# A decode attention kernel: a quarter of the score products moved from TensorE to VectorE, and the exponentials and value products moved later

## The chip, the cores and the metric

One core of a Trainium2 chip runs the kernel. The metric is device time in microseconds (us), with the median over the runs of one kernel. Before the change the kernel took 1358.11 us (median of 4 runs, 1356.54 to 1359.36).

Engine names are those of the profile: PE is TensorE's matmuls, PEld its weight loads, DVE is VectorE, ACT is ScalarE, POOL is GpSimd, and SP issues the large DMA transfers.

## The reference

It is one decode step: one query token against a cache of 65536 keys, with grouped heads, plus a small feed-forward branch.

```python
B, Sq, D = 1, 1, 448
Hq, Hkv, Sk, Dh = 16, 8, 65536, 256      # all bf16
xn = layernorm(x)
q = (xn @ wq)                            # 16 heads of 256
k, v = repeat(k_cache, 2), repeat(v_cache, 2)      # each K/V head serves 2 query heads
p = softmax(q @ k.T * Dh**-0.5)
out = x + (p @ v) @ wo + B(xn)           # B: one gated feed-forward (448 -> 1792 -> 448) on the token
```

The K and V caches are 268 MB each and every byte is used once. Nothing else is near that size: all the weights together are about 12 MB.

## The kernel before

Each of the 8 K/V heads is a head group `g`. Its keys come in 16 chunks of 4096 keys (2 MB of K, 2 MB of V), so there are 128 chunks `i` in all. K and V have three chunk buffers each. One chunk holds 32 tiles of 128 keys.

```python
T = 32; CK = 128 * T; NCH = SK // CK     # 16 chunks per head group
GRP = 4; GPC = T // GRP                  # 8 groups of 4 key tiles per chunk
NKB = 3; NVB = 3; NSLOT = 4; LAG = 3
PV_SLACK = 16
PV_OFF = GPC * NCH + PV_SLACK            # V runs 144 groups = 18 chunks behind K
def _evac_engine(kg): return 1 if (kg % 8) in (2, 6) else 0     # 1: ScalarE, 0: VectorE
```

The kernel first transposes K on TensorE: keys lie on partitions, and the product sums over the 256 head dimensions. For each group it does 8 transposes into a PSUM bank; VectorE or ScalarE copies the bank to SBUF (an eviction, `KTsb`); then TensorE does 8 score products with the two query heads. Scores of a chunk are copied to `Ssb`. The value products of chunk `i - 18` stand between the groups.

```python
# TensorE, for each step n
    if vg % GPC == 0: do_pv_chunk(iv)    # 64 products with V chunk iv
    do_tr(n)                             # 8 transposes of group n
    if n >= LAG: do_qk(n - LAG)          # waits for the eviction of group n-3
```

After 16 chunks VectorE takes the maximum per partition, GpSimd reduces it over partitions, and ScalarE does the exponentials. ScalarE takes its work in program order:

```python
# ScalarE
for kg in range(NG):
    if evac_eng[kg] == 1:
        act.wait_ge(sem_tr, kg + 1)
        ...
        act.copy(KTsb[:, kg % NSLOT, :], kt_ps_bank(kg % NSLOT)).then_inc(sem_eact, 1)
        while exp_next[0] < HKV and kg >= GPC * NCH * (exp_next[0] + 1) + 2:
            do_exp(exp_next[0])          # waits for GpSimd's maximum of that head group
            exp_next[0] += 1
```

SP issues a K chunk when the buffer it goes into is free, that is when all transposes of the chunk three before are done; a V chunk when the products of the V chunk three before are done. `wq` borrows two V buffers at the start.

```python
# SP
if kind == 0:
    if i >= NKB: sp.wait_ge(sem_kfree, i - NKB + 1)
    ... sp.dma_start(Kbuf[:, b, :], src).then_inc(sem_kd[b], 16)
else:
    if i >= NVB: sp.wait_ge(sem_vfree, i - NVB + 1)
    elif b in (0, 1): sp.wait_ge(sem_pe, P_Q)
    ... sp.dma_start(Vbuf[:, b, :], src).then_inc(sem_vd[b], 16)
```

## Time and profile before

| | before |
|---|---|
| span of the profiled run | 1356.7 us |
| busy: PE / DVE / ACT | 81% / 42% / 20% |
| moved by DMA | 552.41 MB |
| DMA rate in most slices | 424 to 428 GB/s |

First the page of the kernel before. The first line is busy time and its share of the span. The next two are the span in 40 equal slices (33.9 us each): the busy share of the 16 DMA engines in tenths, and what they moved. The q lines are DMA queues: packets, MB, share of the 16 engines' time; q8 and q14 fetch the engines' instructions. The L lines are groups of instructions: count, busy time, mean ns of one, and the idle time before them with what ended it.

```profile
PE 1098.2 (81%) x24872; PEld 1069.6 (79%) x24872; DVE 569.6 (42%) x928; ACT 276.7 (20%) x297; POOL 12.2 (1%) x30
...
DMA  9999699999999999999999999999999999999797
GB/s 345 412 411 394 244 427 424 425 425 426 426 424 423 426 405 426 424 424 424 425 425 426 419 374 428 424 423 427 421 426 424 425 422 390 425 425 398 290 417 319
...
q8 instruction: 195, 3.19, 0.9%
q14 instruction: 20, 0.16, 0.0%
...
L473 PE MATMUL ps<-identb,Kbuf 128*128 128x128 bf16 x8192 | 792.5, 254 | 90.7 <-DMA Kbuf<-in_A_k_cache_dram 52.9
L315 DVE COPY KTsb<-ps 128x1024 bf16<-128x1024 bf16 x768 | 521.2, 691 | 513.0 <-PE ps L473 511.0
...
L387 ACT COPY KTsb<-ps 128x1024 bf16<-128x1024 bf16 x256 | 258.9, 1011 | 877.1 <-PE ps L473 877.1
```

PE has the highest busy share of the compute engines, but the DMA row is full and flat. If all 552.41 MB had moved at 425.5 GB/s, it would have taken 1298 us. The span is 59 us longer. As long as the kernel moves these bytes at this rate, only those 59 us can be won, so the first question is where they lie. The Trainium skill (DMA: Bandwidth & Descriptors, "Where 436 GB/s comes from") gives 435.2 GB/s as the ceiling of the 16 ports into SBUF; the flat 424 to 428 GB/s of these slices agrees with being close to it. The same section says that about 358 GB/s, the HBM side, binds for transfers from HBM. It reckons that figure as half of what two cores share; one core alone read 549.03 MB from HBM at 405 GB/s over the whole span here, so for a lone core that limit does not hold in this case.

Next, windows of the kernel before. Columns: the stretch, its length, then busy time and instruction count of each engine, the granted TensorE clock, the DMA engines' busy share, GB/s.

```profile
0.00:60.00 60.00, 28.28 (x391) 23.15 (x392) 13.41 (x25) 5.47 (x10) 7.19 (x14) 1.00 0.96 375
60.00:146.00 86.00, 81.63 (x1984) 80.67 (x1982) 65.17 (x110) 32.00 (x32) 0.00 (x0) 1.00 1.00 402
146.00:180.00 34.00, 22.43 (x517) 22.24 (x515) 13.60 (x24) 8.32 (x11) 0.63 (x2) 0.75 0.64 255
180.00:1240.00 1060.00, 905.25 (x20445) 891.02 (x20443) 466.01 (x751) 225.16 (x237) 3.75 (x12) 0.77 1.00 421
1240.00:1280.00 40.00, 24.33 (x613) 23.80 (x610) 10.59 (x19) 5.76 (x8) 0.63 (x2) 0.64 0.72 286
1280.00:1340.00 60.00, 28.44 (x747) 22.49 (x744) 0.00 (x0) 0.00 (x0) 0.00 (x0) 0.56 1.00 422
1340.00:1356.70 16.70, 7.79 (x198) 6.20 (x198) 0.83 (x3) 0.00 (x0) 0.00 (x0) 0.50 0.49 207
```

I call "time short" the length of a stretch times (1 - its rate / 425.5). It is 7.1, 4.7, 13.6, 11.2, 13.1, 0.5 and 8.6 us for these seven lines, 58.8 us together. In the middle line most of it, 9 us, is in three short holes (slices 15, 23/24 and 34).

The cause of the holes is seen in the timeline around 146 us: start, length, engine, line, instruction, and in brackets the idle time before it and what ended that.

```profile
146.21 0.38 POOL L244 PARTITION_ALL_REDUCE gmax<-pmax  x1 [137.98 <-DVE pmax L307]
148.24 0.61 PE L473 MATMUL ps<-identb,Kbuf 128*128 128x128 bf16 x8
157.47 0.25 POOL L246 TENSOR_SCALAR negmax<-gmax 128x2 f32<-128x2 f32 x1 [10.88 <-issue]
157.75 0.87 ACT L373 ACTIVATE Psb<-Ssb,negmax 128x512 bf16<-128x512 f32 x1 [11.10 <-POOL negmax L246]
159.37 0.99 ACT L387 COPY KTsb<-ps 128x1024 bf16<-128x1024 bf16 x1
160.42 0.37 PE L496 MATMUL ps<-qT,KTsb 128*128 128x2 bf16 x8 [11.57 <-ACT KTsb L387]
```

GpSimd's reduction over partitions takes 11 us here until its result is used (7 to 11 us over the eight head groups). ScalarE reaches the exponential at once and stands there for 11.1 us. The next eviction is behind it in ScalarE's program, and TensorE stands for 11.6 us behind that eviction. All K and V buffers are full then, so the DMA queue stops. The list of waits has this line (total us, times, longest). Seven of the eight are the first seven head groups, with 11.7 us for the first and 4 to 8 us for the others; the eighth is 0.2 us:

```profile
PEld ps L496 <- ACT KTsb L387: 44.0, 8, 11.7
```

### The profile page before, as it was taken

How to read it: one execution, taken by the hardware profiler on the slowest of the kernel's cores; microseconds unless marked ns; L12 is line 12 of the kernel's file. 1: busy time of each engine (PE TensorE's matmuls, PEld its weight loads, DVE VectorE, ACT ScalarE, POOL GpSimd, SP SyncE). 2: the span in 40 equal slices, each digit the busy share in tenths (PEclk: the TensorE clock that was granted, in tenths of full speed). 3: DMA queues.
4: the chain of work that ended last, by engine and by line, in shares of the span. 5: the costliest groups of instructions: out<-in, count | busy, mean ns of one | idle time of the engine just before them, and what ended most of it. 6: DMA issues, size and time to landing. Idle time of an engine off the chain costs nothing.

```text
span 1356.7 us, 52498 instructions
## 1 busy us (share of the span) xinstructions
PE 1098.2 (81%) x24872; PEld 1069.6 (79%) x24872; DVE 569.6 (42%) x928; ACT 276.7 (20%) x297; POOL 12.2 (1%) x30
## 2 busy tenths in 40 slices
PE   3789698897899788887888878898788879888463
PEld 3689698887889788887788878898788879887443
DVE  2378444444444444444444344444344444444100
ACT  0133221222122122212212122221222122121100
POOL 2000000000000000000000000000000000000000
PEclk9999777877777778878877768767788677778565
DMA  9999699999999999999999999999999999999797
GB/s 345 412 411 394 244 427 424 425 425 426 426 424 423 426 405 426 424 424 424 425 425 426 419 374 428 424 423 427 421 426 424 425 422 390 425 425 398 290 417 319
DMA packets 39341, 552.41 MB, mean 407 GB/s; under 512 B 4259, under 2 KB 4294, under 8 KB 5910
## 3 DMA queue, kind: packets, MB, share of 16 engines
q1 hardware_dynamic: 37382, 540.56, 94.9%
q0 software_dynamic: 1744, 8.49, 1.6%
q8 instruction: 195, 3.19, 0.9%
q14 instruction: 20, 0.16, 0.0%
HBM read 549.03 MB, written 0.00 MB: 405 GB/s over the span
## 4 chain that ended last, share of the span: by engine, by line
PE 52%; DMA 35%; issue 9%; ACT 1%; DVE 1%; POOLq 1%; POOL 1%; ACTq 0%
PE ps L473 33%; DMA Kbuf<-in_A_k_cache_dram 27%; PE ps L496 10%; PE ps L529 8%; DMA Vbuf<-in_A_v_cache_dram 4%; DMA wd_sb<-in_B_w_down_dram 3%; POOLq L77 1%; DVE pmax L307 1%; PE ps L551 1%; ACT Psb L373 1%; ACT KTsb L387 1%; PE ps L439 0%; POOL gmax L244 0%; DVE KTsb L315 0%; DVE Ssb L301 0%
## 5 line engine op out<-in xcount | busy, mean ns | idle before, releaser
L473 PE MATMUL ps<-identb,Kbuf 128*128 128x128 bf16 x8192 | 792.5, 254 | 90.7 <-DMA Kbuf<-in_A_k_cache_dram 52.9
L315 DVE COPY KTsb<-ps 128x1024 bf16<-128x1024 bf16 x768 | 521.2, 691 | 513.0 <-PE ps L473 511.0
L473 PEld LDWEIGHTS ps<-identb,Kbuf 128*128 128x128 bf16 x8192 | 594.3, 114 | 94.8 <-DMA Kbuf<-in_A_k_cache_dram 56.9
L387 ACT COPY KTsb<-ps 128x1024 bf16<-128x1024 bf16 x256 | 258.9, 1011 | 877.1 <-PE ps L473 877.1
L496 PE MATMUL ps<-qT,KTsb 128*128 128x2 bf16 x8192 | 374.1, 166 | 61.3 <-ACT KTsb L387 42.1
L496 PEld LDWEIGHTS ps<-qT,KTsb 128*128 128x128 bf16 x8192 | 356.7, 104 | 71.4 <-ACT KTsb L387 44.0
L529 PE MATMUL ps<-Psb,Vbuf 128*128 128x2 bf16 x8192 | 229.4, 164 | 61.4 <-DMA Vbuf<-in_A_v_cache_dram 37.9
L529 PEld LDWEIGHTS ps<-Psb,Vbuf 128*128 128x128 bf16 x8192 | 218.8, 97 | 65.0 <-DMA Vbuf<-in_A_v_cache_dram 38.9
L301 DVE COPY Ssb<-ps 128x64 f32<-128x64 f32 x128 | 28.8, 225 | 134.8 <-PE ps L473 134.4
L336 DVE TENSOR_TENSOR OTsb<-ps,rrec 128x2 bf16<-128x2 f32 x2 | 0.2, 154 | 74.4 <-PE ps L529 74.4
L373 ACT ACTIVATE Psb<-Ssb,negmax 128x512 bf16<-128x512 f32 x16 | 13.4, 859 | 85.2 <-POOL negmax L246 85.2
L421 PE MATMUL ps<-xnT,Vbuf 128*128 128x1 bf16 (+1 forms) x128 | 9.2, 174 | 10.5 <-DMA Vbuf<-in_A_wq_dram 10.5
L421 PEld LDWEIGHTS ps<-xnT,Vbuf 128*128 128x128 bf16 (+1 forms) x128 | 8.3, 106 | 11.4 <-issue 10.5
L244 POOL PARTITION_ALL_REDUCE gmax<-pmax x8 | 3.0, 375 | 1188.5 <-DVE pmax L307 1188.5
L285 DVE TENSOR_TENSOR gs_sb<-ps,sig_sb 128x14 f32<-128x14 f32 x1 | 0.2, 174 | 29.8 <-ACT sig_sb L360 29.8
L439 PE MATMUL ps<-wd_sb,hT_b 128*1 128x448 bf16 x14 | 4.7, 517 | 9.2 <-DMA wd_sb<-in_B_w_down_dram 9.2
L439 PEld LDWEIGHTS ps<-wd_sb,hT_b 128*1 128x1 bf16 x14 | 1.5, 114 | 12.0 <-issue 11.9
L307 DVE TENSOR_REDUCE pmax<-Ssb 128x2 f32<-128x1024 f32 x8 | 9.8, 1220 | 0.3
L551 PE MATMUL ps<-wo_sb,OTsb 128*1 128x448 bf16 x32 | 9.7, 477 | 0.0
L566 PE MATMUL ps<-rowsum,onesf 128*128 128x16 f32 x2 | 0.6, 386 | 11.0 <-ACT Psb L373 11.0
L566 PEld LDWEIGHTS ps<-rowsum,onesf 128*128 128x128 f32 x2 | 0.5, 313 | 11.1 <-ACT Psb L373 11.1
L551 PEld LDWEIGHTS ps<-wo_sb,OTsb 128*1 128x1 bf16 x32 | 3.2, 104 | 5.3 <-issue 4.0
(55 smaller groups left out, 45.9 us busy)
## 6 DMA issues: line engine op xcount, KB each, us to landing
Kbuf<-in_A_k_cache_dram SPq DMA_DIRECT2D x128, 2048.0 KB, 19.9
Vbuf<-in_A_v_cache_dram SPq DMA_DIRECT2D x128, 2048.0 KB, 23.2
wo_sb<-in_A_wo_dram POOLq DMA_DIRECT2D x1, 3584.0 KB, 76.1
Vbuf<-in_A_wq_dram SPq DMA_DIRECT2D x3, 1024.0 KB, 8.2
wd_sb<-in_B_w_down_dram POOLq DMA_DIRECT2D x1, 1568.0 KB, 43.7
wg_sb<-in_B_w_gate_dram POOLq DMA_DIRECT2D x1, 1344.0 KB, 12.7
wu_sb<-in_B_w_up_dram POOLq DMA_DIRECT2D x1, 1344.0 KB, 23.4
Vbuf<-in_A_wq_dram SPq DMA_DIRECT2D x1, 512.0 KB, 16.5
```

The costliest lines, as they stand in the source:

```text
L77: with ExitStack() as es, nc.Block() as block:
L301: dve.tensor_copy(Ssb[:, g % 2, s * 2 * T:(s + 1) * 2 * T], s_ps_chunk(i)).then_inc(sem_sevac, 1)
L307: dve.tensor_reduce(pmax[:, 2 * g:2 * g + 2], sv, AX.X, ALU.max).then_inc(sem_smdve, 1)
L315: dve.tensor_copy(KTsb[:, kg % NSLOT, :], kt_ps_bank(kg % NSLOT)).then_inc(sem_edve, 1)
L373: ins = act.activation(pv[:, h, :], sv[:, h, :], ACTF.Exp, bias=negmax[:, 2 * g + h:2 * g + h + 1], scale=1.0, accum_out=rowsum[:, 2 * g + ...
L387: act.copy(KTsb[:, kg % NSLOT, :], kt_ps_bank(kg % NSLOT)).then_inc(sem_eact, 1)
L421: ins = pe.matmul(ps[:, col:col + 1], lhsT=wq_view(c, kc)[:, h16 * DH + a * 128:h16 * DH + a * 128 + 128], rhs=xnT[0:kc, c:c + 1], start=( ...
L439: ins = pe.matmul(ps[0:1, YC:YC + D_MODEL], lhsT=hT_b[:, f:f + 1], rhs=wd_sb[:, f, :], start=(f == 0), stop=(f == NFC - 1))
L473: ins = pe.transpose(kt_ps(bank, 2 * tl + a), src, identb[:, :])
L496: ins = pe.matmul(s_ps(i2, t), lhsT=KTsb[:, slot, (2 * tl + a) * 128:(2 * tl + a + 1) * 128], rhs=qT[:, a * 16 + 2 * g:a * 16 + 2 * g + 2] ...
L529: ins = pe.matmul(ot_ps(gv, a), lhsT=Vbuf[:, b, t * DH + a * 128:t * DH + a * 128 + 128], rhs=Psb[:, gv % 2, s * 2 * T + 2 * t:s * 2 * T + ...
L551: ins = pe.matmul(ps[0:1, YAC:YAC + D_MODEL], lhsT=OTsb[:, col:col + 1], rhs=wo_sb[:, c, :], start=(first and k == 0), stop=(last and k == ...
```

## The change

It has two parts. First, VectorE scores some key tiles directly: it multiplies 128 keys x 256 values by a q row that lies on every partition and sums along the row (`tensor_tensor_reduce`), which needs neither transpose nor eviction. It takes 4 of 32 tiles in each of the first 19 chunks and 8 of 32 after that. For this, q is computed once more as a row and broadcast to 128 partitions by GpSimd. ScalarE takes all evictions after the 19th chunk. Second, the exponentials come later (11 groups of 6 per chunk into the next chunks, 17 of 7 for the first head group, instead of 2 of 8), and V runs 19 chunks behind K instead of 18. The diff also reorders the start: V chunks 0 and 1, whose buffers hold `wq`, wait for the q row's products too, and V chunk 2 is issued in front of them.

The core of the diff, cut where "..." stands:

```diff
-GPC = T // GRP
-NG = NKCH * GPC
+NTD = [4] * (NCH + 3) + [8] * (NKCH - NCH - 3)          # key tiles of chunk i that VectorE scores
+NTP = [T - n for n in NTD]          # key tiles of chunk i that TensorE scores
+GPCS = [n // GRP for n in NTP]
+G0 = [sum(GPCS[:i]) for i in range(NKCH + 1)]          # first group of chunk i
...
+EXP_AT = 11
+PV_LAG = NCH + 3
...
-    evac_eng = [_evac_engine(kg) for kg in range(NG)]
+    evac_eng = [0 if NTD[CHUNK[kg]] == 4 and (kg - G0[CHUNK[kg]]) in (1, 3, 5) else 1 for kg in range(NG)]
...
                     if i >= NKB:
                         sp.wait_ge(sem_kfree, i - NKB + 1)
+                        sp.wait_ge(sem_ttr, TT0[i - NKB + 1])
...
+            pool.wait_ge(sem_act, A_QROW1)
+            pool.wait_ge(sem_pe, P_GU)
+            pool.partition_broadcast(qb_all, q_row).then_inc(sem_g, 1)
...
+            def dve_scores(i):
...
+                for t in range(NTP[i], T):
+                    for h in range(2):
...                        # evictions of the first 19 chunks, and the scores' copy of chunk i-1, in between
+                        dve.tensor_tensor_reduce(
+                            out=junk((k - 1) % NJUNK), in0=Kbuf[:, b, t * DH:(t + 1) * DH], in1=qb_view(2 * g + h),
+                            scale=1.0, scalar=0.0, op0=ALU.mult, op1=ALU.add,
+                            accum_out=Ssb[:, g % 2, col:col + 1]).then_inc(sem_ttr, 1)
...
-                    while exp_next[0] < HKV and kg >= GPC * NCH * (exp_next[0] + 1) + 2:
+                while exp_next[0] < HKV and kg >= G0[NCH * (exp_next[0] + 1)] + (EXP_AT if exp_next[0] else 17):
...
+            for r in range(2):
...
+                for n4 in range(4):
+                    for c in range(4):
...
+                        ins = pe.matmul(ps[0:1, n4 * BANK:(n4 + 1) * BANK], lhsT=xnT[0:kc, c:c + 1],
+                                        rhs=wq_view(c, kc)[:, n0:n0 + BANK], start=(c == 0), stop=(c == 3))
...
-            for n in range(NG + PV_OFF):
+            for n in list(range(NG)) + [NG + i for i in range(PV_LAG)]:
```

More of the change, by code (lines that the diff above doesn't have):

```diff
@@ L24 @@
 GRP = 4
-GPC = T // GRP
-NG = NKCH * GPC
+NTD = [4] * (NCH + 3) + [8] * (NKCH - NCH - 3)
+NTP = [T - n for n in NTD]
+GPCS = [n // GRP for n in NTP]
+G0 = [sum(GPCS[:i]) for i in range(NKCH + 1)]
+NG = G0[NKCH]
+CHUNK = [i for i in range(NKCH) for _ in range(GPCS[i])]
+TT0 = [2 * sum(NTD[:i]) for i in range(NKCH + 1)]
+EXP_AT = 11
+PV_LAG = NCH + 3
+SE_AT = 8
+NJUNK = 4
 NKB = 3
@@ L30 @@
 LAG = 3
-PV_SLACK = 16
-PV_OFF = GPC * NCH + PV_SLACK
-NVG = NKCH * GPC
 BANK = 512
@@ L47 @@
 OT_BANK0_LAST = 4
-def _evac_engine(kg):
-    return 1 if (kg % 8) in (2, 6) else 0
 def bass_parallel_sum__gqa_block_cached__moe_arch_mod__decode_kernel(
@@ L138, in bass_parallel_sum__gqa_block_cached__moe_arch_mod__decode_kernel @@
         sem_pe = SEM("sem_pe")
+        sem_ttr = SEM("sem_ttr")
         sem_edve = SEM("sem_edve")
@@ L168, in s_ps_chunk @@
             base = (S_BANK0 + (i % 2)) * BANK
-            return ps[:, base:base + 2 * T]
+            return ps[:, base:base + 2 * NTP[i]]
         def ot_bank(g, a):
@@ L182, in bass_parallel_sum__gqa_block_cached__moe_arch_mod__decode_kernel, with qb_view, junk @@
         KC = [128, 128, 128, 64]
+        wu_flat = wu_sb[:, :, :].rearrange("p c f -> p (c f)")
+        wg_flat = wg_sb[:, :, :].rearrange("p c f -> p (c f)")
+        q_row = Ssb[:, :, :].rearrange("p b n -> p (b n)").bitcast(BF16)[0:1, 0:HQ * DH]
+        def qb_view(H):
+            return wu_flat[:, H * DH:(H + 1) * DH]
+        qb_all = wu_flat[:, 0:HQ * DH]
+        def junk(r):
+            return wg_flat[:, HQ * DH + r * DH:HQ * DH + (r + 1) * DH]
         C_XF, C_SUM, C_MEAN, C_XC, C_SQ, C_VS, C_V2, C_RSTD, C_XN, C_XNB, C_WRF, C_RT, C_R, C_ACC, C_GS, C_HT, C_YFFN, C_ACC2, C_RREC, C_OT0, C_OT1, C_OT70, C_OT71, C_FIN = range(1, 25)
-        A_SQRT, A_SIG, A_XNT0, A_XNT1, A_Q, A_SIGG = range(1, 7)
-        P_XNT, P_Q, P_GU, P_Y, P_SUM, P_YATT06, P_YATT = range(1, 8)
+        A_SQRT, A_SIG, A_XNT0, A_XNT1, A_Q, A_QROW0, A_QROW1, A_SIGG = range(1, 9)
+        P_XNT, P_Q, P_QROW0, P_QROW1, P_GU, P_Y, P_SUM, P_YATT06, P_YATT = range(1, 10)
         PROJ_EARLY_CHUNK = NCH * (HKV - 1) + 4
-        G_IOTA, G_IDF, G_IDB, G_ONES = range(1, 5)
+        G_IOTA, G_IDF, G_IDB, G_ONES, G_QB = range(1, 6)
         @block.sync
@@ L199, in _ @@
             for ik in range(NKCH):
-                dep = GPC * (ik - NKB) + GPC - 1 if ik >= NKB else -2
+                dep = 10 * (ik - NKB) + 8 if ik >= NKB else -2
                 items.append((dep, 0, ik))
             for iv in range(NKCH):
-                dep = PV_OFF + GPC * (iv - NVB) if iv >= NVB else -1
+                dep = 10 * (PV_LAG + iv - NVB) if iv >= NVB else (-1.5 if iv == 2 else -1)
                 items.append((dep, 1, iv))
@@ L219, in _ @@
                     elif b in (0, 1):
-                        sp.wait_ge(sem_pe, P_Q)
+                        sp.wait_ge(sem_pe, P_QROW1)
                     src = A_v_cache[0, g, s * CK:(s + 1) * CK, :].rearrange("(p t) d -> p (t d)", p=128)
@@ L300, in s_evac @@
                     dve.wait_ge(sem_exp, g - 1)
-                dve.tensor_copy(Ssb[:, g % 2, s * 2 * T:(s + 1) * 2 * T], s_ps_chunk(i)).then_inc(sem_sevac, 1)
+                dve.tensor_copy(Ssb[:, g % 2, s * 2 * T:s * 2 * T + 2 * NTP[i]], s_ps_chunk(i)).then_inc(sem_sevac, 1)
                 n_sevac[0] += 1
@@ L307, in s_evac @@
                     dve.tensor_reduce(pmax[:, 2 * g:2 * g + 2], sv, AX.X, ALU.max).then_inc(sem_smdve, 1)
-            n_edve = [0]
-            for kg in range(NG):
-                if evac_eng[kg] == 0:
-                    dve.wait_ge(sem_tr, kg + 1)
-                    if kg >= NSLOT:
-                        dve.wait_ge(sem_qk, kg - NSLOT + 1)
-                    dve.tensor_copy(KTsb[:, kg % NSLOT, :], kt_ps_bank(kg % NSLOT)).then_inc(sem_edve, 1)
-                    n_edve[0] += 1
-                    assert n_edve[0] == evac_cnt[kg]
-                if kg % GPC == 1 and kg >= GPC + 1:
-                    s_evac(kg // GPC - 1)
+            n_ttr = [0]
@@ new lines, in dve_scores @@
+            def dve_scores(i):
+                g = i // NCH
+                s = i % NCH
+                b = i % NKB
+                first = True
+                n0 = n_ttr[0]
+                for t in range(NTP[i], T):
+                    for h in range(2):
+                        m = n_ttr[0] - n0
+                        if NTD[i] == 4 and m in (2, 5, 7):
+                            kg = G0[i] + {2: 1, 5: 3, 7: 5}[m]
+                            dve.wait_ge(sem_tr, kg + 1)
+                            if kg >= NSLOT:
+                                dve.wait_ge(sem_qk, kg - NSLOT + 1)
+                            dve.tensor_copy(KTsb[:, kg % NSLOT, :], kt_ps_bank(kg % NSLOT)).then_inc(sem_edve, 1)
+                        if i >= 1 and m == (5 if NTD[i] == 4 else SE_AT):
+                            s_evac(i - 1)
+                        if first:
+                            dve.wait_ge(sem_kd[b], 16 * (i // NKB + 1))
+                            if n_ttr[0] == 0:
+                                dve.wait_ge(sem_g, G_QB)
+                            if s == 0 and g >= 2:
+                                dve.wait_ge(sem_exp, g - 1)
+                            first = False
+                        k = n_ttr[0] + 1
+                        if k > NJUNK:
+                            dve.wait_ge(sem_ttr, k - NJUNK)
+                        col = s * 2 * T + 2 * t + h
+                        dve.tensor_tensor_reduce(
+                            out=junk((k - 1) % NJUNK), in0=Kbuf[:, b, t * DH:(t + 1) * DH], in1=qb_view(2 * g + h),
+                            scale=1.0, scalar=0.0, op0=ALU.mult, op1=ALU.add,
+                            accum_out=Ssb[:, g % 2, col:col + 1]).then_inc(sem_ttr, 1)
+                        n_ttr[0] += 1
@@ new lines, in _ @@
+            for i in range(NKCH):
+                if NTD[i]:
+                    dve_scores(i)
+                    if i >= 1 and NTD[i] != 4 and SE_AT >= 2 * NTD[i]:
+                        s_evac(i - 1)
+                    continue
+                for kg in range(G0[i], G0[i + 1]):
+                    if evac_eng[kg] == 0:
+                        dve.wait_ge(sem_tr, kg + 1)
+                        if kg >= NSLOT:
+                            dve.wait_ge(sem_qk, kg - NSLOT + 1)
+                        dve.tensor_copy(KTsb[:, kg % NSLOT, :], kt_ps_bank(kg % NSLOT)).then_inc(sem_edve, 1)
+                    if i >= 1 and kg == G0[i] + 1:
+                        s_evac(i - 1)
@@ L320, in _ @@
             s_evac(NKCH - 1)
+            assert n_ttr[0] == TT0[NKCH]
             dve.wait_ge(sem_pe, P_SUM)
@@ L358, in _ @@
             inc(act.mul(qT[:, :], ps[:, QC:QC + 32], 1.0 / 16.0), A_Q)
+            for r in range(2):
+                act.wait_ge(sem_pe, P_QROW0 + r)
+                inc(act.mul(q_row[:, r * 4 * BANK:(r + 1) * 4 * BANK], ps[0:1, 0:4 * BANK], 1.0 / 16.0), A_QROW0 + r)
             act.wait_ge(sem_pe, P_GU)
@@ L382, in _ @@
             for kg in range(NG):
-                if evac_eng[kg] == 1:
-                    act.wait_ge(sem_tr, kg + 1)
-                    if kg >= NSLOT:
-                        act.wait_ge(sem_qk, kg - NSLOT + 1)
-                    act.copy(KTsb[:, kg % NSLOT, :], kt_ps_bank(kg % NSLOT)).then_inc(sem_eact, 1)
-                    n_eact[0] += 1
-                    assert n_eact[0] == evac_cnt[kg]
-                    while exp_next[0] < HKV and kg >= GPC * NCH * (exp_next[0] + 1) + 2:
-                        do_exp(exp_next[0])
-                        exp_next[0] += 1
+                if evac_eng[kg] == 0:
+                    continue
+                act.wait_ge(sem_tr, kg + 1)
+                if kg >= NSLOT:
+                    act.wait_ge(sem_qk, kg - NSLOT + 1)
+                act.copy(KTsb[:, kg % NSLOT, :], kt_ps_bank(kg % NSLOT)).then_inc(sem_eact, 1)
+                n_eact[0] += 1
+                assert n_eact[0] == evac_cnt[kg]
+                while exp_next[0] < HKV and kg >= G0[NCH * (exp_next[0] + 1)] + (EXP_AT if exp_next[0] else 17):
+                    do_exp(exp_next[0])
+                    exp_next[0] += 1
             while exp_next[0] < HKV:
@@ L424, in _ @@
             inc(ins, P_Q)
+            for r in range(2):
+                if r == 1:
+                    pe.wait_ge(sem_act, A_QROW0)
+                for n4 in range(4):
+                    for c in range(4):
+                        kc = KC[c]
+                        n0 = r * 4 * BANK + n4 * BANK
+                        ins = pe.matmul(ps[0:1, n4 * BANK:(n4 + 1) * BANK], lhsT=xnT[0:kc, c:c + 1],
+                                        rhs=wq_view(c, kc)[:, n0:n0 + BANK], start=(c == 0), stop=(c == 3))
+                inc(ins, P_QROW0 + r)
             pe.wait_ge(sem_act, A_Q)
@@ L462, in do_tr @@
             def do_tr(kg):
-                ik = kg // GPC
-                grp = kg % GPC
+                ik = CHUNK[kg]
+                grp = kg - G0[ik]
                 b = ik % NKB
@@ L471, in do_tr @@
                             pe.wait_ge(sem_kd[b], 16 * (ik // NKB + 1))
+                            if kg == 0:
+                                pe.wait_ge(sem_act, A_QROW1)
                         src = Kbuf[:, b, t * DH + a * 128:t * DH + a * 128 + 128]
@@ L479, in do_tr @@
                             emit(ins)
-                if grp == GPC - 1:
+                if grp == GPCS[ik] - 1:
                     pending.append((sem_kfree, n_kfree))
             def do_qk(j):
-                i2 = j // GPC
-                grp = j % GPC
+                i2 = CHUNK[j]
+                grp = j - G0[i2]
                 g = i2 // NCH
@@ L504, in do_qk @@
                                 assert n_qk[0] == j + 1
-                                if grp == GPC - 1:
+                                if grp == GPCS[i2] - 1:
                                     pending.append((sem_sfull, n_sfull))
@@ L510, in do_qk @@
                                 emit(ins)
-                                if grp == GPC - 1:
+                                if grp == GPCS[i2] - 1:
                                     pending.append((sem_sfull, n_sfull))
@@ L556, in do_proj @@
                 return ins
-            for n in range(NG + PV_OFF):
-                vg = n - PV_OFF
-                if 0 <= vg < NVG and vg % GPC == 0:
-                    iv = vg // GPC
+            for n in list(range(NG)) + [NG + i for i in range(PV_LAG)]:
+                ik = NKCH + n - NG if n >= NG else CHUNK[n]
+                iv = ik - PV_LAG
+                if iv >= 0 and (n >= NG or n == G0[ik]):
                     if iv == NCH * (HKV - 1):
```

## The prediction

> **What bounds it now.** The DMA queues. The slice table shows the DMA engines 90% or more busy in nearly every slice at 424 to 428 GB/s, and the page gives 552.41 MB moved. At 425.5 GB/s that is 1298 us of the 1356.7 us span. TensorE is busy 81%, but its groups mostly wait for K data; VectorE is busy 42%, ScalarE 20%. So 59 us at most can be won. Windows of the trace place them: 0-60 us (375 GB/s) 7 us; 60-146 us, K only (402) 5 us; 146-180 us (255) 14 us; 180-1240 us (421) 11 us; 1240-1280 us (286) 13 us; 1340 us to the end (207) 9 us.
>
> **Why those dips.** Once per head group ScalarE reaches its exponential about 11 us before GpSimd's maximum is there (chain of waits: 10.8 us "issue", 0.98 us exponential), and its next evacuation of transposed K stands behind it: TensorE waits up to 11.7 us on it, then catches up while K and V buffers stay full. At 146-180 us and three times later this drains the DMA queue. At the end the last exponential comes 11-13 us after the last scores.
>
> **What the change does.** A quarter of the key tiles (an eighth in the first 19 chunks) is scored by VectorE (multiply, sum over 256 elements), so 8192 transposes and 8192 score products fall to about 6300 each. ScalarE takes all evacuations in later chunks (6 x 1.01 us per 9.9 us of DMA time), VectorE 3 of 7 in the early ones. The exponential comes over a chunk and a half after its scores; V lags one chunk more. Added: a q row by 32 wide products (some 0.3 us each; 14 of 448 columns took 4.7 us), two 2048-wide copies (about 1.9 us, from 1.01 us for 1024), and a GpSimd broadcast to 128 partitions.
>
> Cost of a VectorE score, estimated: 448-element f32 tensor-tensor took 0.61 us, so 256 elements about 0.41 us, of which back-to-back copies overlap 0.1 us; the Trainium skill (VectorE: DVE Perf Modes, "Two Vector instructions with no wait between them") says an accumulating op is two instructions, so I add 0.07-0.15 us: 0.38-0.5 us. Sixteen per chunk: 6-8 us, inside 9.9 us. Early: 8 scores + 3 copies + scores' copy, about 5.1-6 us against 4.93 us per K-only chunk, so VectorE is the limit there, about as tight as TensorE's 5.17 us before.
>
> **On the critical path.** Almost none of TensorE's 270 us saved. Gains, in DMA dry time: 146-180 us, 14 to 3; middle, 11 to 3; 1240-1280 us, 13 to 5. Losses: the first VectorE score waits for the broadcast (about 63-69 us, as the GpSimd reductions already take 11 us); chunk 0's buffer comes free about 71 us instead of 58.8: about 10 us. K-only stretch: 0 to 10 us more. Net about -20 us.
>
> **Predicted: 1338 us**, 8 in 10 between 1320 and 1356. Faster by over 2%: 0.32; within 2%: 0.64; slower: 0.04.
>
> **What would show it.** TensorE busy near 65-75%, VectorE 65-80%, ScalarE 45%; DMA still 425 GB/s in the middle, with the mid-run slices at 374-405 GB/s gone; TensorE's waits behind the exponential gone; a new hole near 60-70 us; granted TensorE clock below 0.776, since TensorE idles more (the Trainium skill, TensorE: Matmul & The Clock Gate, Part 1: activity releases the throttle), at no cost.
>
> **What would make it wrong.** VectorE scores over 0.55 us: the limit everywhere. A slow GpSimd broadcast (over 30 us). K buffers freed late by VectorE, running behind TensorE. ScalarE alone too tight for a slow TensorE clock. Or a cheap start: then 1325.

## The result, and the profile after

| | runs | median us | range |
|---|---|---|---|
| before | 16 | 1357.60 | 1352.01 to 1359.69 |
| after | 10 | 1339.24 | 1334.91 to 1343.65 |

The ratio is 0.9873 (95% interval 0.9858 to 0.9887), which is within 2%. Ratios here and below are not quite the ratio of the medians quoted. The profiled run has a span of 1335.3 us, 21.4 us less than the one of before.

The page of the changed kernel, the same parts:

```profile
PE 988.3 (74%) x21112; PEld 953.9 (71%) x21112; DVE 745.2 (56%) x4009; ACT 741.4 (56%) x773; POOL 15.3 (1%) x31
...
DMA  9999999999999999999999999999999999999897
GB/s 337 410 404 404 386 425 424 425 425 425 426 425 425 425 424 425 426 426 425 425 424 425 423 419 423 424 418 417 425 420 423 425 411 424 424 418 394 339 427 321
...
q8 instruction: 165, 2.70, 0.8%
q14 instruction: 49, 0.40, 0.1%
...
L451 ACT COPY KTsb<-ps 128x1024 bf16<-128x1024 bf16 x730 | 720.0, 1016 | 456.7 <-PE ps L549 438.1
L359 DVE CUSTOM_DVE_ANT_0 wg_sb<-Kbuf,wu_sb 128x256 bf16<-128x256 bf16 x1896 | 675.6, 420 | 355.1 <-DMA Kbuf<-in_A_k_cache_dram 355.1
L549 PE MATMUL ps<-identb,Kbuf 128*128 128x128 bf16 x6296 | 678.1, 275 | 261.9 <-DMA Kbuf<-in_A_k_cache_dram 260.3
...
L359 DVE DVE_READ_ACCUMULATOR2_ANT Ssb<- 128x1 f32 x1896 | 155.2, 82 | 0.0
```

The slices at 244, 405, 374 and 390 GB/s are gone. TensorE does 6296 transposes instead of 8192, and its idle time before them that K data ended has grown from 53 to 260 us: it waits for data, as it should. The mean of a transpose is longer (275 against 254 ns), because the granted clock of the whole run fell from 0.776 to 0.712. This fits the Trainium skill (TensorE: Matmul & The Clock Gate, Part 1), which says that activity releases the throttle: TensorE idles more and is granted less. So 15% fewer matmuls (24872 to 21112) saved 10% of TensorE's busy time (1098 to 988 us), and neither figure is the gain in time.

Its windows; the middle ends, and the stretches after it begin and end, 20 us earlier than before, to stay with the same work:

```profile
0.00:60.00 60.00, 38.08 (x375) 22.80 (x376) 12.32 (x31) 10.37 (x14) 9.48 (x15) 0.91 0.97 372
60.00:146.00 86.00, 75.56 (x1763) 74.16 (x1761) 75.99 (x319) 62.75 (x63) 0.00 (x0) 0.96 1.00 399
146.00:180.00 34.00, 28.21 (x655) 27.60 (x652) 26.44 (x129) 24.76 (x27) 0.87 (x2) 0.80 0.99 402
180.00:1220.00 1040.00, 787.60 (x16794) 777.68 (x16792) 615.98 (x3459) 629.91 (x654) 4.29 (x12) 0.69 1.01 423
1220.00:1260.00 40.00, 24.15 (x614) 23.55 (x610) 13.59 (x71) 13.57 (x16) 0.62 (x2) 0.65 0.82 327
1260.00:1320.00 60.00, 27.92 (x769) 22.93 (x770) 0.00 (x0) 0.00 (x0) 0.00 (x0) 0.56 1.01 427
1320.00:1335.30 15.30, 6.80 (x167) 5.20 (x164) 0.83 (x3) 0.00 (x0) 0.00 (x0) 0.50 0.46 195
```

| stretch | time short before | predicted | after |
|---|---|---|---|
| start, to 60 us | 7.1 | 7 plus a hole of 10 near 60 to 70 us | 7.5, no hole |
| K only, to 146 us | 4.7 | 5 to 15 | 5.4 |
| 146 to 180 us | 13.6 | 3 | 1.9 |
| middle | 11.2 | 3 | 6.1 |
| the last 40 us of K | 13.1 | 5 | 9.3 |
| V only and end | 9.1 | not named as changing | 8.1 |

The sum falls from 58.8 to 38.3 us. That is 20.5 us of the 21.4 us between the two spans. The rest is rounding and 0.26 MB less moved.

The timeline of the changed kernel at the start shows two of the costs that the prediction had to estimate:

```profile
50.76 2.30 POOL L261 PARTITION_BROADCAST wu_sb<-Ssb  x1 [42.53 <-ACT sig_sb L423]
...
56.82 0.41 DVE L359 CUSTOM_DVE_ANT_0 wg_sb<-Kbuf,wu_sb 128x256 bf16<-128x256 bf16 x1
57.16 0.07 DVE L359 DVE_READ_ACCUMULATOR2_ANT Ssb<- 128x1 f32 x1
57.16 0.41 DVE L359 CUSTOM_DVE_ANT_0 wg_sb<-Kbuf,wu_sb 128x256 bf16<-128x256 bf16 x1
```

The broadcast took 2.3 us. One VectorE score starts 0.34 to 0.35 us after the one before it: the two instructions of a score overlap with the next one. The Trainium skill's statement that an operation which also writes its accumulator is two instructions (VectorE: DVE Perf Modes, "Two Vector instructions with no wait between them") agrees with the trace: 1896 of 420 ns and 1896 of 82 ns.

In the list of waits of the changed kernel, TensorE's waits behind ScalarE are no longer among the long ones (the last line here). What it and VectorE wait for is K:

```profile
DVE wg_sb L359 <- DMA Kbuf<-in_A_k_cache_dram: 355.1, 106, 5.1
...
PE ps L549 <- DMA Kbuf<-in_A_k_cache_dram: 260.3, 110, 4.3
...
PEld ps L572 <- ACT KTsb L451: 1.8, 2, 1.2
```

### The profile page after: what moved, and what is told of

The parts are those of the page before. It is cut to its first block, busy times and chain, and to the rows that moved or that the text cites. A ratio compares the mean times of both kernels' runs of the same rounds, so it can differ in the third digit from the quotient of the medians.

```text
span 1335.3 us, 48554 instructions
## 1 busy us (share of the span) xinstructions
PE 988.3 (74%) x21112; PEld 953.9 (71%) x21112; DVE 745.2 (56%) x4009; ACT 741.4 (56%) x773; POOL 15.3 (1%) x31
## 4 chain that ended last, share of the span: by engine, by line
DMA 68%; PE 20%; DVE 9%; issue 2%; POOLq 1%; ACT 0%; SPq 0%; POOL 0%; ACTq 0%
DMA Kbuf<-in_A_k_cache_dram 63%; PE ps L549 12%; DVE wg_sb L359 7%; DMA Vbuf<-in_A_v_cache_dram 4%; PE ps L572 3%; PE ps L605 2%; DMA Vbuf<-in_A_wq_dram 1%; PE ps L496 1%; POOLq L80 1%; PE ps L485 1%; PE ps L627 1%; DVE Ssb L321 1%; DVE KTsb L345 1%; PE ps L506 1%; DVE Ssb L359 0%
## 5 line engine op out<-in xcount | busy, mean ns | idle before, releaser
L451 ACT COPY KTsb<-ps 128x1024 bf16<-128x1024 bf16 x730 | 720.0, 1016 | 456.7 <-PE ps L549 438.1
L359 DVE CUSTOM_DVE_ANT_0 wg_sb<-Kbuf,wu_sb 128x256 bf16<-128x256 bf16 x1896 | 675.6, 420 | 355.1 <-DMA Kbuf<-in_A_k_cache_dram 355.1
L549 PE MATMUL ps<-identb,Kbuf 128*128 128x128 bf16 x6296 | 678.1, 275 | 261.9 <-DMA Kbuf<-in_A_k_cache_dram 260.3
L549 PEld LDWEIGHTS ps<-identb,Kbuf 128*128 128x128 bf16 x6296 | 514.3, 124 | 271.5 <-DMA Kbuf<-in_A_k_cache_dram 270.1
L572 PE MATMUL ps<-qT,KTsb 128*128 128x2 bf16 x6296 | 295.5, 168 | 6.4 <-issue 5.5
L572 PEld LDWEIGHTS ps<-qT,KTsb 128*128 128x128 bf16 x6296 | 291.1, 107 | 8.9 <-issue 6.2
L359 DVE DVE_READ_ACCUMULATOR2_ANT Ssb<- 128x1 f32 x1896 | 155.2, 82 | 0.0
L321 DVE COPY Ssb<-ps 128x48 f32<-128x48 f32 (+1 forms) x128 | 26.5, 207 | 88.6 <-PE ps L549 87.3
L345 DVE COPY KTsb<-ps 128x1024 bf16<-128x1024 bf16 x57 | 39.1, 686 | 6.4 <-PE ps L549 6.0
L496 PE MATMUL ps<-Vbuf,xnT 128*1 128x512 bf16 (+1 forms) x32 | 12.4, 513 | 2.0 <-ACT Ssb L421 2.0
L327 DVE TENSOR_REDUCE pmax<-Ssb 128x2 f32<-128x1024 f32 x8 | 9.8, 1220 | 0.3
```

The lines of the kernel that those rows point to most:

```text
L321: dve.tensor_copy(Ssb[:, g % 2, s * 2 * T:s * 2 * T + 2 * NTP[i]], s_ps_chunk(i)).then_inc(sem_sevac, 1)
L345: dve.tensor_copy(KTsb[:, kg % NSLOT, :], kt_ps_bank(kg % NSLOT)).then_inc(sem_edve, 1)
L359: dve.tensor_tensor_reduce(out=junk((k - 1) % NJUNK), in0=Kbuf[:, b, t * DH:(t + 1) * DH], in1=qb_view(2 * g + h), scale=1.0, scalar=0.0, ...
L496: ins = pe.matmul(ps[0:1, n4 * BANK:(n4 + 1) * BANK], lhsT=xnT[0:kc, c:c + 1], rhs=wq_view(c, kc)[:, n0:n0 + BANK], start=(c == 0), stop=( ...
L549: ins = pe.transpose(kt_ps(bank, 2 * tl + a), src, identb[:, :])
L572: ins = pe.matmul(s_ps(i2, t), lhsT=KTsb[:, slot, (2 * tl + a) * 128:(2 * tl + a + 1) * 128], rhs=qT[:, a * 16 + 2 * g:a * 16 + 2 * g + 2] ...
```

## The experiments

The question is which part of the change brought the 18 us. Theory A is the prediction's, put at its sharpest: the gain is the removed wait for the maximum (the exponentials later, V one chunk further back); taking work off TensorE is worth nothing, because the DMA queue sets the pace. Rival B: TensorE must be relieved, so that it can refill the buffers in time. Every kernel that ran gave the correct result.

| run | what | median us | ratio to before, 95% interval |
|---|---|---|---|
| e1 | before + later exponentials and V | 1347.06 | 0.9914 [0.9901, 0.9927] |
| e2 | after, exponentials early again | 1350.06 | 0.9944 [0.9924, 0.9964] |
| e3 | after + six V buffers at the end | 1335.58 | 0.9832 [0.9812, 0.9852] |
| e4 | e1 + six V buffers at the end | 1344.46 | 0.9899 [0.9882, 0.9916] |
| e5 | after, broadcast seven times | 1347.30 | 0.9921 [0.9902, 0.9940] |
| e6 | after, early evictions moved to ScalarE | 1337.26 | 0.9848 [0.9830, 0.9865] |
| e7 | after, VectorE scores in chunks 0 to 18 only | 1346.42 | 0.9914 [0.9898, 0.9930] |
| e8 | after, VectorE scores in chunks 0 to 30 only | 1343.06 | 0.9892 [0.9874, 0.9909] |
| e9 | after, unaltered (control) | 1339.43 | 0.9867 [0.9852, 0.9882] |
| e10 | e3 and e6 together | 1336.64 | 0.9842 [0.9827, 0.9857] |
| e11 | after + 8750 GpSimd memsets | 1362.23 | 1.0027 [1.0014, 1.0041] |
| e12 | after + 8750 GpSimd no-operations | 1360.15 | 1.0009 [0.9991, 1.0027] |

The runs e1 to e4 were made together on one chip, e5 to e8 together, e9 to e11 together, and e12 alone, each with runs of the kernel before beside them.

### e1: the later exponentials alone

```diff
-PV_SLACK = 16
+PV_SLACK = 24
-                    while exp_next[0] < HKV and kg >= GPC * NCH * (exp_next[0] + 1) + 2:
+                    while exp_next[0] < HKV and kg >= GPC * NCH * (exp_next[0] + 1) + (14 if exp_next[0] else 20):
```

> The kernel before, no VectorE scores; only the exponentials come later (20 groups into the next chunks for the first head group, 14 for the others, instead of 2) and V lags one chunk more (19 chunks instead of 18). Theory A (the gain is the removed wait for the maximum; relieving TensorE is worth nothing because the DMA queue sets the pace): the holes at 146-180 us (12 us) and the three mid-run ones (9 us together) go, the tail hole shrinks a little; 1336 to 1342 us, as the changed kernel. Rival B (TensorE must be relieved for the buffers to be refilled in time): 1354 to 1359 us. In between, near 1348: the early, K-only stretch or the catching up needs the relief and the middle does not.

Measured: 1347.06 us. Two thirds of the gain, about 12 us of 18 to 20. The holes behind the exponentials are gone: the windows 480-490, 800-810 and 1120-1130 us, which held the three mid-run holes before (349, 274 and 313 GB/s), are at 422, 426 and 429 GB/s. But the stretch where V joins K is not as good as in the changed kernel. Its window in this run:

```profile
146.00:180.00 34.00, 28.91 (x625) 28.65 (x622) 17.29 (x29) 11.03 (x13) 0.62 (x2) 0.73 0.91 356
```

That is 5.6 us short of full rate, against 1.9 us in the changed kernel. At 170-180 us TensorE is busy all 10 us at a granted clock of 0.50 and the rate is 275 GB/s: with V's products added, a chunk with all 8 groups on a slow TensorE took 9.8 us to free its K buffer (164.4 to 174.2 us). So theory A holds for the larger part and fails for the rest.

### e2: the early exponentials back

```diff
-                while exp_next[0] < HKV and kg >= G0[NCH * (exp_next[0] + 1)] + (EXP_AT if exp_next[0] else 17):
+                while exp_next[0] < HKV and kg >= G0[NCH * (exp_next[0] + 1)] + 2:
```

> The changed kernel with VectorE's scores, but each exponential back at 2 groups after its head group, as before. Theory A: ScalarE again stands 8 to 11 us before each exponential and, as it now does all evacuations, TensorE stops behind it; holes of 5 to 12 us at 150-180 us and small ones later come back: 1348 to 1360 us. Rival B (the gain is TensorE's smaller load, which catches up after a stall before the DMA queue runs dry): 1337 to 1342 us.

Measured: 1350.06 us, 8 us faster than before by the ratio (9 by the medians) and 11 us slower than the changed kernel. The wait came back, as this line of the list of waits of e2 shows (total us, times, longest):

```profile
PEld ps L572 <- ACT KTsb L451: 47.5, 11, 10.2
```

And so did the holes, in two windows of e2 (columns as before), at 273 and 306 GB/s:

```profile
146.00:180.00 34.00, 21.77 (x514) 21.26 (x510) 21.64 (x99) 19.59 (x23) 0.72 (x2) 0.81 0.70 273
790.00:800.00 10.00, 9.37 (x208) 9.20 (x208) 6.26 (x37) 9.78 (x12) 0.00 (x0) 0.74 0.78 306
```

So e1 and e2 split the change into its two parts. The later exponentials alone give a ratio of 0.9914, VectorE's scores with the longer V lag give 0.9944. Their product is 0.9858, and the change measured 0.9873 and 0.9867. Within the intervals the two parts add. Neither theory alone is right: about three fifths of the gain is the timing, two fifths what comes with VectorE's scores. The split is not quite clean: V's longer lag stands in both parts, and the move of the evictions to ScalarE in the second. Neither was tested alone.

### e7 and e8: where the relief counts

```diff
-NTD = [4] * (NCH + 3) + [8] * (NKCH - NCH - 3)
+NTD = [4] * (NCH + 3) + [0] * (NKCH - NCH - 3)                       # e7
+NTD = [4] * (NCH + 3) + [8] * 12 + [0] * (NKCH - NCH - 15)           # e8
-EXP_AT = 11
+EXP_AT = 14
+    # in chunks without VectorE scores, VectorE takes the evictions with (kg - G0[CHUNK[kg]]) % 4 != 2
```

> The changed kernel, but VectorE scores keys only in the first 19 (K-only) chunks; later chunks go as in the kernel before, all on TensorE, with evictions three of four on VectorE; the late exponentials stay. If TensorE's relief counts only in the K-only stretch: 1338 to 1342 us. If it counts at the change to K and V together (a chunk on a slow-clocked TensorE takes 9.8 us there without VectorE's scores) or in the steady middle: 1344 to 1348 us.

> As the run before, with VectorE scoring eight key tiles also in the 12 chunks after the K-only stretch, and none in the 97 after that. If the relief counts only where buffers must be caught up, at the change from K alone to K and V: 1338 to 1342 us, as the changed kernel. If the steady middle needs it too: 1342 to 1347 us.

Measured: e7 1346.42 us, e8 1343.06 us. The run e7 equals e1, which has no VectorE scores at all (0.9914 both). So VectorE's scores in the K-only stretch, with the q row, the broadcast and eight scores per chunk, bring nothing that the runs resolve (some 2 us). Twelve more chunks of scores bring 3.4 us: in e7 the stretch 160-180 us runs at 374 GB/s, in e8 at 424 (first line e7, second e8). That is the change from K alone to K and V together.

```profile
160.00:180.00 20.00, 15.40 (x315) 15.19 (x316) 5.93 (x10) 5.55 (x8) 0.00 (x0) 0.61 0.95 374
160.00:180.00 20.00, 16.05 (x380) 15.73 (x381) 12.34 (x71) 13.58 (x16) 0.00 (x0) 0.74 1.00 424
```

The other 97 chunks bring the last 4 us, from 1343.06 to 1339. The intervals of e8 and of the control e9 overlap (0.9874 to 0.9909 against 0.9852 to 0.9882), so these 4 us are at the edge of what the runs resolve.

The last 4 us are not a hole. In e8 the windows 700-1000 and 1000-1200 us run at 419 and 420 GB/s, in the changed kernel at 422 and 421, and the DMA engines are 100 to 101% busy in both. What differs is how long packets take. A 16 KB packet of K or V takes 0.61 to 0.62 us nearly always. Counted from the packets in the traces, from 700 to 1200 us 2.2 to 2.3% of them take over 0.7 us in e8, 2.4 to 2.5% in e1, 1.6 to 1.7% in the changed kernel, and 1.0 to 1.1% in the kernel before and in e2. Between 200 and 400 us it is 0.7% in all of them. So where the holes went away, part of what they had cost came back as longer packets. Why they are fewer with VectorE's scores is not shown.

### e11 and e12: is it the fetching of instructions?

The change takes 52498 instructions down to 48554. Instructions are fetched by the same DMA engines (queues q8 and q14), and the Trainium skill (DMA: Bandwidth & Descriptors, "Queues, rings and completion order") says that each engine goes round its queues packet by packet. If a fetch costs more than its bytes, fewer instructions would explain the last 4 us. Both runs add instructions that do no useful work, 1250 after each of the first seven maxima:

```diff
                 pool.tensor_single_scalar(negmax..., -1.0, ALU.mult).then_inc(sem_pool, 1)
+                for m in range(1250 * g, 1250 * g + (1250 if g < HKV - 1 else 0)):      # e11
+                    if m >= 16:
+                        pool.wait_ge(sem_pad, m - 15)
+                    pool.memset(scratch[0:1, m % 16:m % 16 + 1], 0.0).then_inc(sem_pad, 1)
+                for m in range(1250 if g < HKV - 1 else 0):                             # e12
+                    pool.engine_nop()
```

> The changed kernel with 8750 idle one-element GpSimd memsets added, spread over the run: work for nobody, but over twice the 4000 instructions that the change saves, which the instruction queue must fetch through the same DMA engines. Theory C (the 4 us that VectorE's scores bring in the steady middle come from fewer TensorE instructions to fetch, each fetch throwing the 16 DMA engines out of step): 6 to 10 us slower than the control, and more than 2% of K and V packets over 0.7 us after 700 us. Rival (only the fetched bytes count, 0.56 MB or about 1.3 us; the packets' stretching has another cause): 0 to 3 us slower, fraction 1.5 to 1.8% as now.

> As the last run, but with 8750 no-operations on GpSimd in place of the memsets: as many instructions to fetch, with no write and no semaphore. Theory C (instructions fetched beside a full DMA queue cost far more than their bytes): again 15 to 23 us slower than the changed kernel, 1354 to 1362 us. Rival D (it was the memsets' writes or their 8750 semaphore updates): 1338 to 1343 us, the fetched bytes being worth 1.3 us.

Measured: 1362.23 and 1360.15 us, 23 and 21 us slower than the changed kernel. Since no-operations cost as much as memsets, neither the writes nor the semaphores are the cause; what both have in common is the instructions. From the page of e12, with q14 against 49 packets and 0.40 MB in the changed kernel:

```profile
GB/s 353 409 393 411 389 422 426 424 426 422 425 425 426 423 404 415 425 425 423 404 410 422 425 422 384 412 424 425 414 383 407 426 423 415 378 422 389 288 422 318
...
q14 instruction: 117, 0.96, 0.2%
```

The dips stand where the bursts of no-operations are, from the third burst on, and spread past their ends. From 700 to 1200 us 3.4 to 3.7% of the K and V packets take over 0.7 us. The 0.56 MB more would take 1.3 us at 425.5 GB/s; the cost is 21 us, or 0.3 us for each of the 68 more fetches. It is shown that instructions cost that much beside a full DMA queue. That it is their fetching is argued: each run lists a span and a clock, so recording was likely on, a no-operation is recorded as well (57304 instructions in the trace), and no run separates fetching from executing or recording.

The traces give a lead that I did not test. The q14 packets took 40.4 us together in e12, 42.4 us in e11 and 16.3 us in the changed kernel. So the 68 more fetches took 24 and 26 us of DMA engine time, about what the runs lost. If they all went through one of the 16 engines, that engine would finish its share of K and V that much later than the others. The end of K looks like it: from 1260 to 1264 us the DMA engines are 9% busy in e12 and 8% in e11, which is one or two of 16. The middle (180 to 1240 us) loses some 17 us against the changed kernel, and 4 us more are lost at 1240-1280 us, after the last no-operation. The trace does not name the engine of a packet, so this stays an estimate.

It is not shown that this explains the last 4 us of VectorE's scores. The change fetches fewer packets on q8 (195 to 165) but more on q14 (20 to 49), about as many in sum, and the runs do not say what one of q8 costs. By instructions alone, an estimate from e12 (21 us for 8750) would give 8 us for the 3395 instructions between e8 and the changed kernel, twice what is measured. Why the cost grows along the run (the first two bursts cost almost nothing) stays open too; an engine that falls behind a little with each fetch, until the queued chunks no longer hide it, would fit.

### e5: a late first score

```diff
-            pool.partition_broadcast(qb_all, q_row).then_inc(sem_g, 1)
+            for rep in range(7):
+                if rep:
+                    pool.wait_ge(sem_g, G_ONES + rep)
+                pool.partition_broadcast(qb_all, q_row).then_inc(sem_g, 1)
-                                dve.wait_ge(sem_g, G_QB)
+                                dve.wait_ge(sem_g, G_ONES + 7)
```

> The changed kernel with the GpSimd broadcast of q done seven times in a row, so that VectorE's first score waits until about 67 us (2.3 us each) instead of starting at 57 us: the lateness that my prediction had expected. If the step of the prediction holds (a late first score holds up the first K buffer while all that was queued has landed, and the DMA queue runs dry): a hole near 60 to 72 us and about 8 us more, 1345 to 1350 us. Rival (there is slack at the start, which later K-only chunks make good): 1338 to 1342 us.

Measured: 1347.30 us, 8 us slower than the changed kernel. The first K buffer came free at 70.6 us instead of 61.5, and the hole is where it was expected. This window of e5 is to be read against 406 GB/s in the same window of the changed kernel:

```profile
60.00:70.00 10.00, 2.74 (x44) 2.75 (x45) 4.18 (x17) 0.39 (x1) 5.49 (x3) 0.50 0.69 257
```

So the mechanism of that step of the prediction is right and lateness at the start is not made good later. Only the broadcast is much quicker than assumed.

### e6: is VectorE the limit in the K-only stretch?

```diff
-... (kg - G0[CHUNK[kg]]) in (1, 3, 5) ...
+... (kg - G0[CHUNK[kg]]) in (1, 4) ...
-                        if NTD[i] == 4 and m in (2, 5, 7):
-                            kg = G0[i] + {2: 1, 5: 3, 7: 5}[m]
+                        if NTD[i] == 4 and m in (2, 6):
+                            kg = G0[i] + {2: 1, 6: 4}[m]
```

> The changed kernel; in the first 19 chunks ScalarE takes five of the seven evictions of transposed K instead of four, VectorE two instead of three. If VectorE's work (8 scores of 0.345 us, 3 copies of 0.6 us, one small copy: about 4.8 us, with gaps 5.1) is what sets the K-only pace: VectorE 4.3 us per chunk, and the stretch 60-160 us gains up to 3 us: 1336 to 1338 us. If the DMA queue or TensorE sets it: no change, 1338 to 1342 us.

Measured: 1337.26 us, which by the median is 2 us under the changed kernel and by the interval can't be told from it. The profile decides better: VectorE's busy time in 60-146 us fell from 76.0 to 67.5 us, and the rate of that stretch is 402 GB/s, against 399 in the changed kernel and 403 in the control e9. VectorE is not the limit there. With the DMA engines 99 to 100% busy at 399 to 403 GB/s, and 6 to 8% of the K packets over 0.7 us, the DMA queue is, at a lower rate than later. Why packets are longer in this stretch stays open.

### e3, e4, e9 and e10: the last 40 us of K

In the changed kernel the stretch 1220-1260 us is 9.3 us short. V has three buffers, and each new V chunk waits for a value product that waits for the last K chunks, or for the last exponential. K's three buffers fall free just then. The edit gives V chunks 111 to 127 both kinds of buffers:

```diff
+# V chunk iv: the buffer it is loaded into (K's buffers are free at the end), and what that buffer held before
+VPREV = [("v", iv - NVB) for iv in range(NKCH)]
+VPREV[NKCH - 17:NKCH - 12] = [("k", NKCH - 3), ("v", NKCH - 20), ("k", NKCH - 2), ("v", NKCH - 19), ("k", NKCH - 1)]
+VPREV[NKCH - 12:] = [("v", iv - 6) for iv in range(NKCH - 12, NKCH)]
...
-                        sp.wait_ge(sem_vfree, i - NVB + 1)
+                        if VPREV[i][0] == "v":
+                            sp.wait_ge(sem_vfree, VPREV[i][1] + 1)
+                        else:
+                            sp.wait_ge(sem_kfree, VPREV[i][1] + 1)
+                            sp.wait_ge(sem_ttr, TT0[VPREV[i][1] + 1])
```

> The changed kernel; only V chunks 111 to 127 differ: the three K buffers, free at the end, take V chunks as well, so V is fetched up to six chunks ahead while the last maximum and exponential are awaited. My theory of the last 40 us of the K stretch (9 us short of full rate because V has only three buffers, each freed by a product that waits for the last K chunks or the last exponential): that hole falls from 9 us to under 2; 1329 to 1333 us. Rival (the rate falls there for another reason, as the end of the K stream or the memory itself): 1337 to 1342 us.

> The kernel before with the later exponentials and V lag of the first run and the six-deep V buffers of the third, without VectorE scores. Theory A: the two gains add and VectorE's scores are not needed: 1328 to 1334 us, under the changed kernel. Rival B: 1345 us or more.

Measured: e3 1335.58 us, about 4 us under the changed kernel, where 6 to 10 were expected; e4 1344.46 us, 2.6 us under e1. The hole itself did close. These are windows of e3:

```profile
1220.00:1260.00 40.00, 23.47 (x556) 22.95 (x553) 13.59 (x71) 14.10 (x17) 0.62 (x2) 0.61 1.00 407
...
1315.00:1325.00 10.00, 3.88 (x139) 3.72 (x137) 0.00 (x0) 0.00 (x0) 0.00 (x0) 0.50 0.56 238
```

It runs at 407 GB/s where the changed kernel has 327. But a new stretch stands at the end: for 10 us the DMA engines are 56% busy, which is 9 of 16. Some engines have finished and the others have 10 us of their share left. In the changed kernel nearly the same, 57%, stands at 1227-1230 and 1237-1242 us. So part of the hole seems never to have been waste: the engines that were behind caught up in it, and it was only the others that stood. A sum of bytes over a common rate does not see this. The 10 us at 56% are worth 4.4 us, about what is missing to the expected gain. Which engines are behind, and by what, the traces don't name.

The miss in e4 is the same as in e1: it lacks what VectorE's scores bring.

> The changed kernel unaltered, as a control for the two runs beside it on the same chip: 1337 to 1341 us, ratio to before 0.986 to 0.989.

> The changed kernel with the six-deep V buffers of the third run and the five-of-seven ScalarE evictions of the sixth. If the two gains (3 to 4 us and 2 to 3 us) are real and independent: 1331 to 1335 us, 5 to 7 us under the control. If the second was chance: 1334 to 1337 us.

Measured: the control is 1339.43 us, the two edits together (e10: `VPREV` as in e3, evictions as in e6) 1336.64 us. That is 3 us under the control and not better than e3 alone, so the evictions of e6 bring nothing and the second alternative of the expectation holds. The six-deep V buffers give a version that beats both kernels by the medians, e3 at 1335.58 us. Its interval (0.9812 to 0.9852) just touches that of the control (0.9852 to 0.9882), so a gain of 3 to 4 us over the change is likely and at the edge of what the runs resolve.

## Why the prediction was right or wrong

The time was predicted as 1338 us and measured as 1339.24 us, within 2% of before, as said to be the likeliest. Point by point:

- **The bound is the DMA queue, with at most 59 us to win: right.** The rate in the middle stayed at 425 GB/s or just below, however the work was spread.
- **The holes come from the wait for the maximum: right.** In e1 the later exponentials alone remove them and give 12 us; in e2 putting them back costs 11 us. 146 to 180 us was predicted to go from 14 to 3 and went to 1.9.
- **"Almost none of TensorE's 270 us saved" on the critical path: true to the letter, misleading for the gain.** This is the weakest step of the mechanism. By e1 and the changed kernel, VectorE's scores bring 8 us. That is 3% of 270 us, but two fifths of the 18 to 20 us gained, where the prediction names only the removed wait as the cause of the holes. e7 and e8 place them: none in the K-only stretch, 3.4 us where V joins K and the buffers must be refilled by a TensorE at half clock, 4 us spread over the middle, with an open cause. Nor were 270 us of TensorE's time saved; its busy time fell by 110 us, as its clock fell too.
- **The start, 10 us lost: wrong by its size.** The broadcast was put at some 15 us, from the 11 us of GpSimd's reductions, and took 2.3 us. With a broadcast as late as assumed, e5 loses 8 us. The mis-sized term is the broadcast.
- **VectorE as the limit in the K-only stretch: not confirmed.** A score took 0.345 us from start to start instead of 0.38 to 0.5, and e6 shows that taking work off VectorE does not raise the rate.
- **The middle, 11 to 3, and the last 40 us of K, 13 to 5: too hopeful.** They came to 6.1 and 9.3. In the middle longer packets took the place of part of the holes; at the end part of the hole was DMA engines catching up (e3).
- **The sum.** The terms as written add up to a gain of 27 us and losses of 10 to 20 us, so 7 to 17 us, not the "about -20 us" beside them. So the number is closer than its reasons. Measured term by term, in the order of the stretches in the table of time short, 11.7 + 5.1 + 3.8 + 1.0 us were gained (146 to 180 us, the middle, the last 40 us of K, V only and the end), and 0.4 + 0.7 us lost (the start, K only): 20.5 us. The total came out right because the loss at the start did not happen, which made up for the 7 us of gain that the middle and the end of K fell short by, and for the slip in the addition. That it came so close is luck.
- **Signs in the profile.** TensorE 74% (65 to 75 said), clock 0.712 (below 0.776 said), no long wait behind the exponential: right. VectorE 56% (65 to 80% said) and ScalarE 56% (45% said): wrong, the first by the cost of a score, the second against the prediction's own terms (6 copies of 1.01 us in 9.9 us are 61%). A hole near 60 to 70 us: absent.

## What to carry to other kernels

When a kernel streams at the memory's pace, list the stretches where the stream falls below it and price a change only there; then ask which engine's in-order queue stands in front of the stream in each. An instruction that waits for a slow result belongs later in its queue, behind work that others need, and that can be had without moving any arithmetic. A right total proves little about its terms: test the halves of a change separately, as e1 and e2 do.

## What the Trainium skill lacked or had wrong

- No page has the price of fetching instructions beside a full DMA queue. 8750 GpSimd no-operations, 0.56 MB of fetches in 68 packets, cost 21 us (e12), where the bytes alone would take 1.3 us. It would belong to Runtime: NRT & Kernel Launch, in "Instruction fetch mechanics".
- GPSIMD Engine Reference gives no time for a broadcast to all partitions or a small reduction over partitions. Here a 4096-element bf16 row took 2.3 us to broadcast, and the maximum of 128 x 2 values 7 to 11 us until its result was used.
- VectorE: DVE Perf Modes, "The DRAIN you can't avoid", says that the next operation does not start until the pipe is empty, except one that is not held, which starts earlier; it does not say by how much. Here scores of 420 ns start every 345 ns, with the accumulator read of 82 ns in between, so successive operations overlap in the record.
- DMA: Bandwidth & Descriptors, "Where 436 GB/s comes from", says without a condition that the HBM side at about 358 GB/s binds for transfers from HBM. The page's table of measured bandwidth, just above, limits this to both cores of an HBM domain streaming. One core alone ran at 424 to 428 GB/s for most of 1.3 ms here, so the sentence needs that condition.
- No page says how far the 16 DMA engines can drift apart within a stream; DMA: Bandwidth & Descriptors, "Latency and other measured facts", only calls engines 7 and 15 usually slower. At the end of e3 the engines were 56% busy for 10 us, as if 9 of 16 worked that much longer than the others.
